# Accumulating DMAs for every third weight chunk only; VectorE subtracts for the others

## The chip, the cores and the metric

One core of one Trainium2 chip runs the whole program. The time is the device time of one execution in microseconds; the kernel before stands at a median of 909.94 us over three executions (907.95 to 910.76).

## What is computed

Three layers in a row on 2304 tokens of 512 features, all in float32. First random-feature attention with 8 heads of 64 features over 4 batches of 576 tokens, then a gated network, then a routed one with 8 experts (one for each token).

```python
q_p, k_p = (phi(q_s), phi(k_s))          # phi: exp(x @ omega.T - |x|^2/2 - max) / sqrt(128)
kv = np.einsum('bhsm,bhsd->bhmd', k_p, v)
num = np.einsum('bhsm,bhmd->bhsd', q_p, kv)      # divided by its normaliser
...
g = x @ w_gate                                   # w_gate, w_val: 512 x 1536, w_out: 1536 x 512
silu = g * (1.0 / (1.0 + np.exp(-g)))
val = x @ w_val
x = silu * val @ w_out
...
out[mask] = gate_w[mask, None] * (np.maximum(x[mask] @ w1[e], 0.0) @ w2[e])
```

The weights w_gate, w_val and w_out arrive as float64. "Chunk" means 128 rows by 512 columns of one of them; there are 36.

## The kernel before

*Precision.* A float32 product is made of three fast TensorE products: each operand is split in a high part, rounded to the engine's fast format (fp32r), and a low part, the rest (`mm3`, lines 169 to 171; `split`, lines 174 and 175). A weight chunk therefore needs a high and a low tile.

*Stages.* Tokens go in 6 groups of 3 tiles of 128. The first stage does three things at once: the attention of batch 0 and of the first group (16 "units" of one tile and four heads, of kind k or q), the conversion of all 36 weight chunks, and, as soon as the six q units are done, the gated network of group 0, together with 14 units for group 1. The gated network runs over f = 0 to 11 (128 hidden features each): 24 products into gv (four w_gate chunks, four w_val chunks), the gating (`gate`, lines 932 to 947, on ScalarE and VectorE), and 9 products into acc with a w_out chunk. f needs the chunks of its quarter f // 4. The other groups follow with the next group's units between their products, then the expert network in 10 slots.

*A chunk's steps* (`wsteps`, line 402). SP loads 512 KB of float64 into a w tile (line 400). Then a, b, c on VectorE (lines 414, 418, 422) put the bits of a float32 together out of the two integer halves, in a temporary tile t. d writes the high part, on VectorE for the first six chunks (line 428, NH = 6), on ScalarE for the others (line 430). e, on ScalarE, writes -t into the low tile, rounded (line 434). f, on GpSimd's queue, issues a DMA that adds t to the low tile (line 437), so that t minus its rounded value is left. The temporary t is one of three "row" buffers, or, for a "roomy" chunk (n % 5 >= 3 and n < 30, RM = (5, 3, 30)), a tile of the large pool "w" of 37. It is given back when the DMA has landed.

*The order.* Within the first stage it is planned ahead of time. `Plan` (line 84) holds steps with an engine, an assumed duration, the steps they wait for, the buffers they take and give, and a rank. `Plan.run` picks again and again the step that can start first by its own clock, and among those that start within 0.02 us the one with the lowest rank, and writes out its instructions. Every engine executes its own instructions in that order. The ranks are lines: chunk n has CR + CS n (23.68 + 8.39 n), its load CD + 1.4 n, a load waits for step c of the chunk WP = 5 before; the start's k units have 0 to 9 and q units RQ + RS i (7.83 + 1.56 i); the next group's unit i has UR + UD i (73.3 + 6.7 i); f has MR + MS f (44.22 + 15.56 f). The loads for the next group's units are issued by `pump`, first at rank PU = 2.0 and again each time a unit gives a load buffer back (`freed`, line 300). All loads are on SP's queue, in the planned order. The planner takes an accumulating DMA for 1.5 us and a lag of 2.4.

Behind the first stage the order comes from due times that don't depend on the plan. GpSimd also has the small bias operations (lines 536, 537) that the exponentials (line 546) wait for.

Of the kernel before, what the change touches and what calls it, by code (L numbers as in the profile page):

```python
# [8 lines left out]
F32 = mybir.dt.float32  # L9
# [3 lines left out]
ALU = mybir.AluOpType  # L13
# [15 lines left out]
FO = 5.72  # L29
FC = 0.6  # L30
MD = (0, 0, 0.17, 1.8, 2.18)
QL = -1.2
QD = 0.26
LAT = 0.34
GRAIN = 0.02
CR = 23.68
CD = -8.87
CS = 8.39
UR = 73.3
UD = 6.7  # L40
MR = 44.22
MS = 15.56
NH = 6
RR = 94.76
XL = 16.71
WU = 4
GF = 0
OR = 0
EO = 3.84
RQ = 7.83  # L50
RS = 1.56
PU = 2.0
WP = 5
RM = (5, 3, 30)
MXB = 4
US = 5.61
P = 128
# [64 lines left out]
def kernel(  # L122
# [16 lines left out]
    nc = tc.nc  # L139
# [33 lines left out]
    def split(src, hi, lo):  # L173
        nc.scalar.copy(hi, src)  # L174
        nc.vector.tensor_tensor(out=lo, in0=src, in1=hi.bitcast(F32), op=ALU.subtract)  # L175
# [7 lines left out]
    with tc.manual_schedule():  # L183
# [72 lines left out]
        def edge(t):  # L256

            return len(segs(t)) > 1
# [123 lines left out]
        wch = {}  # L382
# [9 lines left out]
        def wload(n):  # L392
            key = worder[n]
            r = wraw[key] = wpool.tile([P, DM, 2], I32, tag="w", name="wraw")
            if key[0] == "o":
                src = w_out[key[1] * P:(key[1] + 1) * P, :]
            else:
                src = (w_gate if key[0] == "g" else w_val)[
                    key[1] * P:(key[1] + 1) * P, key[2] * 4 * P:(key[2] + 1) * 4 * P]
            nc.sync.dma_start(out=r.rearrange("p c w -> p (c w)"), in_=src.bitcast(I32))  # L400

        def wsteps(key, by_dve, roomy):

            st = {}


            def a():
                st["r"] = wraw.pop(key)

                if roomy:  # L410
                    st["t"] = wpool.tile([P, 2 * DM], I32, tag="w", name="wt")[:, 0:DM]
                else:
                    st["t"] = rows.tile([P, DM], I32, tag="row", name="wt")
                nc.vector.tensor_scalar(out=st["t"], in0=st["r"][:, :, 1], scalar1=3, scalar2=0x3FFFFFFF,
                                        op0=ALU.logical_shift_left, op1=ALU.bitwise_and)

            def b():
                nc.vector.scalar_tensor_tensor(out=st["t"], in0=st["r"][:, :, 1], scalar=-0x40000000, in1=st["t"],
                                               op0=ALU.bitwise_and, op1=ALU.bitwise_or)

            def c():
                nc.vector.scalar_tensor_tensor(out=st["t"], in0=st["r"][:, :, 0], scalar=29, in1=st["t"],
                                               op0=ALU.logical_shift_right, op1=ALU.bitwise_or)

            def d():
                wch[key] = wpool.tile([P, 2, DM], F32R, tag="w", name="w")
                if by_dve:
                    nc.vector.tensor_copy(wch[key][:, 0, :], st["t"].bitcast(F32))
                else:
                    nc.scalar.copy(wch[key][:, 0, :], st["t"].bitcast(F32))  # L430


            def e():
                nc.scalar.mul(wch[key][:, 1, :], st["t"].bitcast(F32), -1.0)

            def f():
                nc.gpsimd.dma_start(out=wch[key][:, 1, :], in_=st["t"].bitcast(F32), accum_op=ALU.add)

            return a, b, c, d, e, f


        kv_sb = {}
# [274 lines left out]
        for g0, g1, nstat in ((0, NG - 1, 8), (NG - 1, NG, 2)):  # L717
# [3 lines left out]
            n = r.nt * P  # L721
# [431 lines left out]
        def start_unit(i, at, offs):  # L1153
            for n, f in unit_stages(i).items():
                T.at(at + offs[n], f)

        plan = Plan(dict(gv=2, acc=GT, misc=2, row=3, vt=4, h=2, xh=1, th=1, u=2, kvp=1, w=33),
                    dict(pe=LAT, act=LAT, dve=LAT, pool=LAT, dma=1.7, wadd=2.4))
        dur = dict(T=0.34, xh=0.26, sq=0.7, ss=0.42, pj=0.87, rd=0.7, md=0.4, ex=1.01, kv=0.83, ko=0.42, kw=0.43,
                    kp=0.42, qt=0.43, qc=0.39, nm=0.87, dv=1.09, xt=0.22, hi=0.27, lo=0.34)  # L1160
        on = dict(T="pe", xh="act", sq="act", pj="pe", rd="dve", ex="act", kv="pe", ko="act", kw="pe", kp="act", qt="pe", qc="act", nm="pe",
# [12 lines left out]
        def load_chunk(n):  # L1174
            back = chunk[n - WP][2] if n >= WP else None
            got["w", n] = plan.add("dma", 1.46, lambda: wload(n), [back], CD + 1.4 * n, ["w"])

        def load_q(n):
            loads[n] = first_x(n)
# [6 lines left out]
        where = {}  # L1186
        for n, key in enumerate(worder):
            load_chunk(n)
            roomy = n % RM[0] >= RM[1] and n < RM[2]
            st = wsteps(key, n < NH, roomy)  # L1190
            room1 = ["w" if roomy else "row"]
            c = []
            for f, (eng, d) in zip(st + (lambda: None,), (("dve", 0.34), ("dve", 0.61), ("dve", 0.61), ("dve", 0.34) if n < NH else ("act", 0.52), ("act", 0.53), ("pool", 0.9), ("wadd", 1.5))):
                c.append(plan.add(eng, d, f, [c[-1] if c else got["w", n]], CR + CS * n,
                                  room1 if f is st[0] else ["w"] if f is st[3] else [],
                                  ["w"] if f is st[2] else room1 if eng == "wadd" else []))
            chunk.append(c)
            where[key] = c[6]
        kvs = []
        ends = {}  # L1200
        on.update(sq="pool", ss="dve", md="pool")
# [3 lines left out]
        om_split = plan.add("act", 0.3, lambda: split(om_f, om_h, om_l), [], OR)  # L1205
        pumped = plan.add("dma", 1.6, pump, [got["edge", 1]], PU)
        for i in range(nu):
            kind, t, j = units[i]
            step = {"kvs": None, "kvt": None, "v": None}
            early = i < n_start  # L1210
            rank = UR + (i - n_start) * UD if not early else i if kind == "k" else RQ + RS * (i - 10)
            if not early:
                back = {k: ends[i - k] if i - k >= n_start else None for k in (2, 3)}
                step["x"] = plan.add("dma", 1.6, lambda: None, [back[3], pumped], rank)
            elif kind == "q":
                step["x"] = plan.add("dma", 0.8, lambda n=i: load_q(n), rank=QL + QD * (i - 10), take=["w"])
                step["kvs"], step["kvt"] = kvs[j]
# [6 lines left out]
            for n, f in unit_stages(i).items():  # L1224
                d = 0.43 if n == "kv" and edge(t) else dur[n]
                nd, eng = needs[n], on[n]
                if not early and n in ("sq", "md"):
                    nd, eng, d = (["T"], "act", 1.9) if n == "sq" else (["rd", "sq"], "pool", dur["md"])
                if not native and n == "pj":
                    nd, d = nd + [om_split], 0.65  # L1230
                if not native and n == "xh":
                    d = 0.6
# [26 lines left out]
        ra, rb, rc, rd = route_setup()  # L1259
        s = plan.add("dma", 0.5, later_loads, [s], XL)  # L1260
        s = plan.add("dve", 0.14, ra, [s], RR)
        s = plan.add("pe", 0.05, rb, [s], RR, ["misc"])
        s = plan.add("dve", 0.1, rc, [s], RR, [], ["misc"])
        plan.add("dve", 0.75, rd, [s], RR, [], ["w"])
        plan.run(ready[-1])
# [3 lines left out]
        for f in range(NF):  # L1269
            rank = MR + MS * f  # L1270
            s = half["v", 0] if f else ready[-1]
# [14 lines left out]
            if f:  # L1286
                s = half["v", 1]
                for i in range(GT):
                    s = plan.add("pe", 0.69, lambda f=f, i=i: l2(f - 1, i), [us[f - 1], where["o", f - 1, 0], s], rank,
                                 ["acc"] if f == 1 else [], ["u"] if i == GT - 1 else [])  # L1290
        plan.add("pe", 0.4, turn_gate, [], MR + 75)
        fin = plan.add("end", 0, lambda: None, [us[-1], s])
# [19 lines left out]
        st = slot_prefetch(A, 0, tf + PF, PD, tf + 2.6 * FO + FC * 11 + PG)  # L1312
        moe1_group(NG - 1)
        cur = pending[0]
        for i, (r, s) in enumerate(slots):
# [5 lines left out]
            st = nst  # L1321
# [57 lines left out]
```

## Time and profile before

| | us |
|---|---|
| median of three executions | 909.94 |
| profiled execution, device time | 909.23 |
| its span, first to last instruction | 907.5 |
| TensorE busy (matmul) | 866.2 |
| VectorE busy | 599.5 |
| ScalarE busy | 403.5 |
| GpSimd busy | 120.5 |

How to read it: "busy" counts the time in which at least one instruction of an engine runs. A view by stretch tells where an engine stood still, a view of waits names for each idle time the instruction that ended it (the one that ended it last by the records, which can be one that was itself held up), and the chain of work that ended last goes back from the end, at each step to what released it. PEclk is TensorE's granted clock as a share of 2.4 GHz. L414 means line 414; PE is TensorE, DVE VectorE, ACT ScalarE, POOL GpSimd. "w<-wt" is the accumulating DMA, "wraw<-in_..." a chunk's load.

### The profile page before, as it was taken

To read this page: it belongs to the slowest core of one execution; us is meant where nothing else is said; L and a number is where in the kernel's file an instruction comes from. 1 tells how busy PE (TensorE), PEld (TensorE's weight loads), DVE (VectorE), ACT (ScalarE), POOL (GpSimd) and SP (SyncE) were. 2 spreads that over 40 slices of the span, in tenths; PEclk is the share of its full clock that TensorE was granted. 3 is DMA by queue.
4 is the path that set the end of the run, shared out by engine and by line. 5 is a ranking of instruction groups with operands and counts; after the bars stand their busy time and mean duration, and the time that the engine had idled before them with its cause. 6 is when DMAs were issued, how large, how long until landed. Compare 5 with 4: busy or idle time off the path is not lost.

```text
span 907.5 us, 15212 instructions
## 1 busy us (share of the span) xinstructions
PE 866.2 (95%) x5320; PEld 799.5 (88%) x5320; DVE 599.5 (66%) x1535; ACT 403.5 (44%) x1101; POOL 120.5 (13%) x251
## 2 busy tenths in 40 slices
PE   7888689999999999999999999999999999999993
PEld 6777589999999999999999999999999999999992
DVE  5888558457665667655666665488787788766630
ACT  4777458543333334243343331112455555555520
POOL 6833133100000000000000000000201111112100
PEclk9999799999999999999999999999999999999997
DMA  9969894221222212222111111124587776676400
GB/s 266 268 160 263 205 263 85 42 63 43 59 76 63 55 35 53 47 81 55 35 42 45 45 28 36 47 82 140 163 325 251 243 238 223 221 236 216 137 19 22
DMA packets 96913, 112.89 MB, mean 124 GB/s; under 512 B 54176, under 2 KB 56242, under 8 KB 96827
## 3 DMA queue, kind: packets, MB, share of 16 engines
q1 hardware_dynamic: 88171, 92.35, 33.1%
q0 software_dynamic: 8384, 19.40, 9.2%
q8 instruction: 44, 0.72, 0.3%
q14 instruction: 42, 0.34, 0.1%
q10 hardware_dynamic: 272, 0.07, 0.0%
HBM read 92.91 MB, written 9.98 MB: 113 GB/s over the span
## 4 chain that ended last, share of the span: by engine, by line
PE 71%; issue 12%; DMA 9%; POOL 3%; DVE 2%; SPq 1%; ACT 1%; POOLq 0%; DVEq 0%
PE gv L169 10%; PE gv L171 10%; PE gv L170 10%; PE acc L169 7%; PE acc L170 7%; PE acc L171 7%; DMA w<-wt 3%; DMA out_dram<-orow,sidx 3%; PE num L601 3%; PE h L171 2%; PE h L170 2%; PE h L169 2%; DMA wraw<-in_moe_w_gate_dram 2%; PE kv L568 1%; PE qt L592 1%
## 5 line engine op out<-in xcount | busy, mean ns | idle before, releaser
L169 PE MATMUL gv<-xT,w 128*128 128x384 f32 x576 | 202.6, 352 | 2.8 <-DVE th L935 2.6
L171 PE MATMUL gv<-xT,w 128*128 128x384 f32 x576 | 194.8, 338 | 0.6 <-DMA w<-wt 0.6
L170 PE MATMUL gv<-xT,w 128*128 128x384 f32 x576 | 194.7, 338 | 0.0
L169 PE MATMUL acc<-w,uh 128*128 128x512 f32 x360 | 147.8, 410 | 0.0
L170 PE MATMUL acc<-w,uh 128*128 128x512 f32 x360 | 142.6, 396 | 0.0
L171 PE MATMUL acc<-w,ul 128*128 128x512 f32 x360 | 142.1, 395 | 0.0
L546 ACT ACTIVATE h<-pr,mx 128x128 f32<-128x128 f32 x224 | 63.9, 368 | 143.9 <-DVE mx L541 127.1
L169 PEld LDWEIGHTS gv<-xT,w 128*128 128x128 f32 x576 | 109.2, 190 | 7.7 <-DVE th L935 3.8
L170 PEld LDWEIGHTS gv<-xT,w 128*128 128x128 f32 x576 | 109.3, 190 | 2.9
L175 DVE TENSOR_TENSOR w<-raw,w 128x512 fp32r<-128x512 f32 x160 | 106.4, 686 | 6.1 <-ACT w L174 2.3
L171 PEld LDWEIGHTS gv<-xT,w 128*128 128x128 f32 x576 | 109.0, 189 | 0.9 <-DMA w<-wt 0.9
L747 DVE SCALAR_TENSOR_TENSOR wge<-xrow,wge 128x512 f32<-128x512 f32 x144 | 98.6, 684 | 10.1 <-DMA wge<-wg2t 9.5
L174 ACT CAST w<-raw 128x512 fp32r<-128x512 f32 x160 | 92.8, 617 | 4.6 <-DMA raw<-in_moe_w_dram 4.6
L169 PE MATMUL h<-sx,w 128*128 128x256 f32 x320 | 91.6, 286 | 0.0
L171 PE MATMUL h<-sx,w 128*128 128x256 f32 x320 | 90.5, 283 | 0.0
L170 PE MATMUL h<-sx,w 128*128 128x256 f32 x320 | 90.4, 283 | 0.0
L171 PEld LDWEIGHTS acc<-w,ul 128*128 128x128 f32 x360 | 68.0, 189 | 15.6 <-DVE ul L1095 0.2
L169 PEld LDWEIGHTS acc<-w,uh 128*128 128x128 f32 x360 | 68.5, 190 | 7.3
L170 PEld LDWEIGHTS acc<-w,uh 128*128 128x128 f32 x360 | 68.6, 190 | 7.0
L944 ACT CAST uh<-th 128x384 fp32r<-128x384 f32 x72 | 37.6, 522 | 67.5 <-DVE th L939 67.3
L525 DVE TENSOR_REDUCE mx<-pr 128x4 f32<-128x512 f32 x72 | 49.5, 688 | 26.1 <-PE pr L171 22.1
L169 PEld LDWEIGHTS h<-sx,w 128*128 128x128 f32 x320 | 61.0, 190 | 3.1
(196 smaller groups left out, 1434.7 us busy)
## 6 DMA issues: line engine op xcount, KB each, us to landing
raw<-in_moe_w_dram SPq DMA_DIRECT2D x80, 512.0 KB
wge<-wg2t SPq DMA_DIRECT2D x48, 256.0 KB
w<-wt POOLq DMA_DIRECT2D x36, 256.0 KB, 6.3
wraw<-in_moe_w_gate_dram SPq DMA_DIRECT2D x12, 512.0 KB
wraw<-in_moe_w_val_dram SPq DMA_DIRECT2D x12, 512.0 KB
wraw<-in_moe_w_out_dram SPq DMA_DIRECT2D x12, 512.0 KB
scr<-xrow SPq DMA_DIRECT2D x18, 256.0 KB
xin<-in_q_dram SPq DMA_DIRECT2D x26, 128.0 KB
```

The source lines that it names most:

```text
L169: nc.tensor.matmul(o, lh, rh, start=start, stop=False, skip_group_check=True)
L170: nc.tensor.matmul(o, lh, rl, start=False, stop=False, skip_group_check=True)
L171: nc.tensor.matmul(o, ll, rh, start=False, stop=stop, skip_group_check=True)
L174: nc.scalar.copy(hi, src)
L175: nc.vector.tensor_tensor(out=lo, in0=src, in1=hi.bitcast(F32), op=ALU.subtract)
L525: nc.vector.tensor_reduce(out=mx, in_=pr, axis=AX.X, op=ALU.max)
L546: nc.scalar.activation(out=h[:, a, :], in_=pr[:, a, :], func=ACTF.Exp, bias=mx[:, a:a + 1])
L568: nc.tensor.matmul(kv_ps[0][:, g, :], h[:, c, :], vt[:, c, 0:D + 1], start=t == own[0] and c == 0, stop=t == own[-1], skip_group_check=True)
L592: nc.tensor.transpose(qt[:, h, :], st["h"][:, h, :], ident)
L601: nc.tensor.matmul(num[r:r + m, h, :], st["h"][:, h, r:r + m], kv_sb[b, j][:, h, :], start=True, stop=True)
L747: nc.vector.scalar_tensor_tensor(out=st[e][:, 1, :], in0=xrows[i], scalar=1.0, in1=st[e][:, 0, :], op0=ALU.mult, op1=ALU.mult, accum_out=L ...
L944: nc.scalar.copy(u[f][0], th[f])
```

## The change

For chunks with n % 3 = 1 (12 of 36) all steps stay as they are, with the high part on ScalarE. For the other 24, steps e and f fall away, and VectorE writes the low part as t minus the high part ("low"). Temporary tiles out of the w pool are now for accumulating chunks with n < 30 only (ten of them); a temporary tile of a chunk without a DMA is given back behind "low". The high part is on ScalarE for all chunks. The planner's assumed lag of the DMA goes from 2.4 to 3.0, and the ranks of the first stage have other values.

```diff
--- before.py
+++ after.py
@@ -29,29 +29,28 @@
 FO = 5.72
 FC = 0.6
 MD = (0, 0, 0.17, 1.8, 2.18)
-QL = -1.2
-QD = 0.26
+QL = -1.24
+QD = 0.41
 LAT = 0.34
 GRAIN = 0.02
-CR = 23.68
-CD = -8.87
-CS = 8.39
-UR = 73.3
-UD = 6.7
-MR = 44.22
-MS = 15.56
-NH = 6
-RR = 94.76
-XL = 16.71
+CR = -3.19
+CD = -8.51
+CS = 8.62
+UR = 68.99
+UD = 9.09
+MR = 46.53
+MS = 29.47
+RR = 106.64
+XL = 17.9
 WU = 4
 GF = 0
 OR = 0
 EO = 3.84
-RQ = 7.83
-RS = 1.56
-PU = 2.0
+RQ = 7.32
+RS = 2.67
+PU = 9.84
 WP = 5
-RM = (5, 3, 30)
+RM = (3, 1, 30)
 MXB = 4
 US = 5.61
 P = 128
@@ -399,7 +398,7 @@
                     key[1] * P:(key[1] + 1) * P, key[2] * 4 * P:(key[2] + 1) * 4 * P]
             nc.sync.dma_start(out=r.rearrange("p c w -> p (c w)"), in_=src.bitcast(I32))
 
-        def wsteps(key, by_dve, roomy):
+        def wsteps(key, by_dma, roomy):
 
             st = {}
 
@@ -424,10 +423,11 @@
 
             def d():
                 wch[key] = wpool.tile([P, 2, DM], F32R, tag="w", name="w")
-                if by_dve:
-                    nc.vector.tensor_copy(wch[key][:, 0, :], st["t"].bitcast(F32))
-                else:
-                    nc.scalar.copy(wch[key][:, 0, :], st["t"].bitcast(F32))
+                nc.scalar.copy(wch[key][:, 0, :], st["t"].bitcast(F32))
+
+            def low():
+                nc.vector.tensor_tensor(out=wch[key][:, 1, :], in0=st["t"].bitcast(F32),
+                                        in1=wch[key][:, 0, :].bitcast(F32), op=ALU.subtract)
 
 
             def e():
@@ -436,7 +436,7 @@
             def f():
                 nc.gpsimd.dma_start(out=wch[key][:, 1, :], in_=st["t"].bitcast(F32), accum_op=ALU.add)
 
-            return a, b, c, d, e, f
+            return (a, b, c, d, e, f, lambda: None) if by_dma else (a, b, c, d, low)
 
 
         kv_sb = {}
@@ -1155,7 +1155,7 @@
                 T.at(at + offs[n], f)
 
         plan = Plan(dict(gv=2, acc=GT, misc=2, row=3, vt=4, h=2, xh=1, th=1, u=2, kvp=1, w=33),
-                    dict(pe=LAT, act=LAT, dve=LAT, pool=LAT, dma=1.7, wadd=2.4))
+                    dict(pe=LAT, act=LAT, dve=LAT, pool=LAT, dma=1.7, wadd=3.0))
         dur = dict(T=0.34, xh=0.26, sq=0.7, ss=0.42, pj=0.87, rd=0.7, md=0.4, ex=1.01, kv=0.83, ko=0.42, kw=0.43,
                     kp=0.42, qt=0.43, qc=0.39, nm=0.87, dv=1.09, xt=0.22, hi=0.27, lo=0.34)
         on = dict(T="pe", xh="act", sq="act", pj="pe", rd="dve", ex="act", kv="pe", ko="act", kw="pe", kp="act", qt="pe", qc="act", nm="pe",
@@ -1186,16 +1186,19 @@
         where = {}
         for n, key in enumerate(worder):
             load_chunk(n)
-            roomy = n % RM[0] >= RM[1] and n < RM[2]
-            st = wsteps(key, n < NH, roomy)
+            by_dma = n % RM[0] == RM[1]
+            roomy = by_dma and n < RM[2]
+            st = wsteps(key, by_dma, roomy)
             room1 = ["w" if roomy else "row"]
             c = []
-            for f, (eng, d) in zip(st + (lambda: None,), (("dve", 0.34), ("dve", 0.61), ("dve", 0.61), ("dve", 0.34) if n < NH else ("act", 0.52), ("act", 0.53), ("pool", 0.9), ("wadd", 1.5))):
+            on_w = [("dve", 0.34), ("dve", 0.61), ("dve", 0.61), ("act", 0.52)]
+            on_w += [("act", 0.53), ("pool", 0.9), ("wadd", 1.5)] if by_dma else [("dve", 0.61)]
+            for f, (eng, d) in zip(st, on_w):
                 c.append(plan.add(eng, d, f, [c[-1] if c else got["w", n]], CR + CS * n,
                                   room1 if f is st[0] else ["w"] if f is st[3] else [],
-                                  ["w"] if f is st[2] else room1 if eng == "wadd" else []))
+                                  ["w"] if f is st[2] else room1 if f is st[-1] else []))
             chunk.append(c)
-            where[key] = c[6]
+            where[key] = c[-1]
         kvs = []
         ends = {}
         on.update(sq="pool", ss="dve", md="pool")
```

## Rows read from the trace of the kernel before

**Rows 1.** Busy time by stretch: us, each engine's busy us, granted clock, DMA share.
```profile
0.00:182.00 182.00, 156.38 (x933) 138.84 (x934) 125.48 (x278) 114.47 (x386) 74.14 (x180) 0.95 0.77 193
8.00:60.00 52.00, 42.84 (x270) 35.76 (x269) 42.99 (x98) 37.34 (x130) 36.06 (x98) 0.99 0.91 231
8.00:131.00 123.00, 101.24 (x579) 88.10 (x579) 92.30 (x197) 78.01 (x262) 58.09 (x135) 0.93 0.93 242
60.00:90.00 30.00, 27.52 (x159) 25.49 (x158) 24.29 (x48) 18.74 (x56) 11.31 (x17) 0.97 0.95 254
93.70:100.30 6.60, 0.00 (x1) 0.00 (x0) 2.55 (x7) 0.09 (x1) 0.39 (x2) 0.68 1.11 254
100.30:107.00 6.70, 6.68 (x25) 6.11 (x26) 4.42 (x12) 4.30 (x17) 0.10 (x1) 0.55 0.59 112
125.60:131.00 5.40, 5.37 (x24) 4.91 (x25) 2.76 (x5) 3.82 (x12) 1.45 (x3) 0.68 1.05 360
131.00:182.00 51.00, 50.87 (x342) 47.23 (x342) 31.30 (x72) 33.38 (x118) 12.29 (x24) 1.00 0.39 71
182.00:880.00 698.00, 698.00 (x4324) 650.55 (x4323) 471.70 (x1251) 287.16 (x711) 44.37 (x69) 1.00 0.35 111
```

**Rows 2.** Waits of TensorE, 59.9 to 182 us: total us, times, longest.
```profile
PE xt L483 <- DVE setup L690: 6.6, 1, 6.6
PE gv L169 <- DVE th L935: 2.6, 3, 1.2
PE pr L169 <- DVE xl L175: 2.3, 1, 2.3
PE gv L171 <- DMA w<-wt: 0.6, 1, 0.6
```

**Rows 3.** VectorE in order of time: start, length, idle time before and its releaser.
```profile
97.75 0.76 DVE L414 TENSOR_SCALAR wt<-wraw 128x512 int32<-128x512 int32 x2 [6.96 <-DMA w<-wt]
...
122.42 0.43 DVE L414 TENSOR_SCALAR wt<-wraw 128x512 int32<-128x512 int32 x1 [1.92 <-DMA w<-wt]
```

**Rows 4.** Chain of work that ended last: start us, length us, what.
```profile
85.99 11.73 DMA w<-wt
```

**Rows 5.** Groups of instructions, 0 to 182 us: count, busy us, mean ns, idle before.
```profile
L437 POOL DMA_DIRECT2D w<-wt x36 | 31.9, 952 | 28.9 <-ACT w L434 25.9 <-issue 0.9 <-ACT xT L623 0.7
...
L422 DVE SCALAR_TENSOR_TENSOR wt<-wraw,wt 128x512 int32<-128x512 int32 x36 | 25.5, 712 | 0.1
...
L418 DVE SCALAR_TENSOR_TENSOR wt<-wraw,wt 128x512 int32<-128x512 int32 x36 | 24.5, 684 | 0.2
...
L434 ACT ACTIVATE w<-wt 128x512 fp32r<-128x512 f32 x36 | 22.7, 652 | 0.0
...
L430 ACT CAST w<-wt 128x512 fp32r<-128x512 f32 x30 | 18.1, 635 | 5.6 <-DVE wt L422 5.6
...
L414 DVE TENSOR_SCALAR wt<-wraw 128x512 int32<-128x512 int32 x36 | 15.9, 454 | 17.2 <-DMA w<-wt 14.5 <-DMA wraw<-in_moe_w_val_dram 2.8
...
L428 DVE CAST w<-wt 128x512 fp32r<-128x512 f32 x6 | 2.5, 412 | 0.0
```

**Rows 6.** Group of instructions in the page: the expert weights' subtraction.
```profile
L175 DVE TENSOR_TENSOR w<-raw,w 128x512 fp32r<-128x512 f32 x160 | 106.4, 686 | 6.1 <-ACT w L174 2.3
```

**Rows 7.** Waits of VectorE for ScalarE, 182 to 907 us.
```profile
DVE xl L175 <- ACT xh L174: 36.4, 35, 2.1
...
DVE w L175 <- ACT w L174: 2.3, 2, 1.3
```

**Rows 8.** SP's DMA issues in order of time around its gap.
```profile
85.39 0.87 SPq L400 DMA_DIRECT2D wraw<-in_moe_w_gate_dram  x1
...
103.79 0.38 SPq L253 DMA_DIRECT2D xin<-in_k_dram  x1
```

**Rows 9.** GpSimd in order of time, two equal products.
```profile
32.81 0.61 POOL L497 TENSOR_TENSOR first<-first 128x256 f32<-128x256 f32 x1
...
34.99 0.91 POOL L497 TENSOR_TENSOR first<-first 128x256 f32<-128x256 f32 x1
```

## The prediction

> **What bounds the kernel now.** I read the busy time by stretch first [rows 1]. From 182 to 880 us TensorE is busy for 698.00 of 698.00 us at a granted clock of 1.00, so behind 182 us only less TensorE work would help, and the edit doesn't touch that: it changes the planner's input, and the planner writes out only the first stage, whose last matmul ends at 182 us. Between 131 and 182 us TensorE is busy too (50.87 of 51.00 us). Whatever there is to win lies before 131 us: it stands still for all of 93.7 to 100.3 us and for 2.5 of the 30 us from 60 to 90, and the clock is 0.55 and 0.68 of full speed in two stretches, each just behind a standstill: a mix of 2.4 GHz and 1.2 GHz.
>
> Next the list of TensorE's waits from 59.9 to 182 us [rows 2]: 6.6, 2.6, 2.3 and 0.6 us, 12.1 in all. The name beside the largest (VectorE's setup, line 690) is not its cause. VectorE's queue [rows 3] shows a chunk's first step (line 414) that starts at 97.75 us after 6.96 us of waiting for an accumulating DMA; line 690 and a row maximum merely stood behind it. The chain of waits [rows 4] has that DMA with 11.73 us from 85.99. The mechanism is the row buffer: three of them, each held by a chunk until its accumulation has landed, and VectorE runs in order. The 2.3 us are of the same kind: a step of line 414 waits 1.92 us up to 122.42 [rows 3], and the xl that TensorE needs comes after it.
>
> A slow clock costs 6.70 x 0.45 = 3.0 us, 5.40 x 0.32 = 1.7 and 30 x 0.03 = 0.9 [rows 1], together 5.6. So TensorE alone could end the stage at 182 - 12.1 - 5.6 = 164.3 us. Of these 17.7 us, 6.6 + 2.3 + 0.6 + 3.0 + 1.7 = 14.2 go back to accumulating DMAs.
>
> **The change part by part.** *Accumulations.* 24 of 36 go (chunks with n % 3 = 1 keep theirs). With each goes a negation on ScalarE and an issue on GpSimd: 24 x 0.652 = 15.6 us and 24 x 0.952 = 22.8 us [rows 5]. On GpSimd's queue stand the small bias operations that the exponentials wait for, so they come forward; what that is worth before 60 us I bound below. A chunk without a DMA gives its row buffer back when VectorE itself has subtracted, so the next line 414 never waits for another engine on its account. Of the 12 accumulating chunks ten now take a w tile (n < 30), and only n = 31 and 34 hold a row buffer. A third of 14.2 us would be 4.7; as two chunks of 12 can still block a row, I leave 2 us of it in the time, between 0 and 4.7.
>
> *VectorE.* The subtraction isn't in the trace for these tiles; the same one, 128x512 fp32r out of two SBUF operands, takes 0.686 us 160 times later on [rows 6]. 24 x 0.686 = 16.5 us come; six hi copies of 0.412 [rows 5], 2.5 us, move to ScalarE, where they take 0.635 each. VectorE's work up to 182 us grows from 125.5 [rows 1] to 139.5 us. None of that is hidden for certain: VectorE is the engine that takes over the bound. In 8 to 131 us it is idle for 123 - 92.3 = 30.7 us [rows 1]; line 414's waits for the accumulation and for one load explain 14.5 + 2.8 [rows 5], and 13.4, or 11%, are left as ordinary gaps. With 11% gaps the new work ends at 8 + 139.5 / 0.89 = 164.7 us, as good as TensorE's 164.3. At the occupancy of 8 to 60 us, 42.99 of 52 or 83%, it would be 8 + 139.5 / 0.83 = 176.
>
> *The new wait.* Each subtraction waits for ScalarE's hi copy of its chunk. Behind it on VectorE stand the next chunks, the row maxima and the gating of the first expert network, so GpSimd, ScalarE and TensorE wait for it in turn. The nearest pairs: the same copy and subtraction in the later stages cost 2.3 us for 160 pairs, 0.01 each, and xl behind its xh in the steady stage 36.4 us over 35 waits, 1.04 each, where VectorE has time to spare [rows 7]. I take 0.15 each, near the lower end, as the planner puts other work between copy and subtraction: 24 x 0.15 = 3.6 us, between 0.2 and 25.
>
> *The start, up to 60 us.* The rank of chunk 0 falls from 23.68 to -3.19, so chunks 0 to 2 (-3.19, 5.43, 14.05) may go ahead of attention units (0 to 9, and 7.32 to 20.67). Price: at most three chunks of 0.454 + 0.684 + 0.712 + 0.686 = 2.5 us, 7.6 us of VectorE [rows 5, 6], of which idle time (17% of the stretch) takes some. Against it GpSimd, busy for 36.06 of the 52 us [rows 1], loses two in three of its 0.952 us issues there. I bound the sum by 4 us either way and take 0.
>
> *Ranks and load order.* Units of the next group now go ahead of f of the expert network earlier (29.47 per f, before 15.56), and the pump of their loads stands behind some six more chunk loads (9.84, before 2.0, at 1.4 per chunk). On SP's queue a unit's load can hold the chunk loads behind it: between 85.39 and 103.79 us it issued nothing [rows 8]. VectorE lost only 2.8 us to a chunk load so far [rows 5]; between a gain of 2.8 and the 17.5 us of that blockade I take 0, since most of the chunks are on chip before they are wanted.
>
> *Sum.* 164.5 + 3.6 + 2 = 170.1 us for the end of the stage, 12 us before 182. The profiled execution took 909.23 us (span 907.5 and 1.73 around it; 0.7 under the median of 909.94): 909.23 - 12 = 897.
>
> *A rule that speaks against it.* GpSimd's 128x256 product takes 0.61 us at 32.81 us and 0.91 at 34.99, while VectorE converts a chunk [rows 9]. The Trainium skill (page "SBUF — State Buffer", section "SBUF: two separate sides") says why that can be: a VectorE operation with two SBUF inputs and a GpSimd operation that reads SBUF exclude one another for the whole instruction. The new subtraction has two SBUF inputs, so the rule would have each of the 24 hold GpSimd back by up to its length, an estimated 2 us on the path if one in eight hits a bias operation, and the sum would be 899 instead of 897.
>
> **The rivals.**
> - TensorE alone is left as the bound: the subtractions never wait, and the start gains its 4 us. For it: both ends come to 164.5 us already. Against it: VectorE would have to run at 139.5 of 156 us, 89%, throughout. 909.23 - 17.7 - 2 to 4 = 888.
> - VectorE waits for ScalarE (slower). In-order VectorE stands at each subtraction until ScalarE, itself held by exponentials that wait for GpSimd and so for VectorE's row maxima, has copied. At the 1.04 us of xl [rows 7] the stage ends at 164.5 + 25 + 2 = 191.5, 9.5 us later: 919. It decides from (182 - 164.5 - 2) / 24 = 0.65 us a subtraction. For it: VectorE loses its slack. Against it: 0.01 us in 160 equal pairs.
> - The loads give it back (no change). SP's blockade of 17.5 us [rows 8] moves to where VectorE has emptied the stock of loaded chunks; 12 to 15 us of that come back, 907 to 910. For it: chunks are used up faster, their loads don't start faster. Against it: 2.8 us so far.
> - The edit does what it says in any case: the 24 issues are absent from the program. What may not come is the release of the row buffers, if chunks 31 and 34 alone block as before; that is the 4.7 us above.
>
> **How the numbers follow.** Forecast (stage ends at 165 to 179 us) 0.61; TensorE alone 0.14; VectorE waits 0.15; loads 0.10. 0.3%, 2.7 us, is about what a measurement of this kernel tells from no change. Faster: 0.61 + 0.14 = 0.75; the loads case gives 0.08 to no change and 0.02 to slower; slower 0.17. The range runs from the first rival with the start's 4 us (909.23 - 17.7 - 4 = 887) to the middle of the loads case, 908: 0.61 + 0.14 + half of 0.10 = 0.80.
>
> **What would show it.** Right: line 414 no longer waits for the accumulation by more than about 2 us in sum; no standstill of TensorE over 3 us behind 60 us; clock near 1.00 throughout the stage; VectorE busy for about 139 us in it; last matmul of group 0 at about 170 us, and the rest as long as before. Wrong: VectorE's subtractions wait for ScalarE by more than 0.65 us each (second rival); line 414 waits for chunk loads by 10 us or more (third); TensorE begins the expert network clearly after 60 us, so that the start pays for the new ranks; or the stretch behind the stage changes its length.

## The result and the profile after

The changed kernel takes 893.99 us (median of four, 893.12 to 895.30) where the kernel before takes 910.2: a ratio of 0.9828, 95% interval 0.9806 to 0.9849. The profiled execution takes 894.53 us with a span of 892.8, against 909.23 and 907.5: 14.7 us less.

The busy time by stretch divides these 14.7 us (columns as in [rows 1]). First the kernel before, cut where TensorE begins the first step of the next stage, a transposition of line 483 (182.89 us), and where its last product ends (891.86):

```profile
0.00:182.89 182.89, 157.27 (x937) 139.55 (x938) 125.60 (x279) 114.84 (x387) 74.14 (x180) 0.95 0.77 192
182.89:891.86 708.97, 708.96 (x4384) 659.90 (x4382) 472.85 (x1253) 288.63 (x714) 45.36 (x70) 1.00 0.35 109
891.86:907.50 15.64, 0.00 (x0) 0.00 (x0) 1.03 (x4) 0.00 (x0) 0.98 (x1) 0.59 0.06 15
```

And the changed kernel, cut at the same two steps:

```profile
0.00:170.46 170.46, 154.84 (x937) 138.05 (x938) 136.07 (x297) 106.04 (x369) 56.76 (x156) 0.98 0.62 170
170.46:879.59 709.13, 709.13 (x4384) 660.20 (x4382) 472.88 (x1252) 288.66 (x714) 46.33 (x70) 1.00 0.35 109
879.59:892.80 13.21, 0.00 (x0) 0.00 (x0) 1.03 (x4) 0.00 (x0) 0.98 (x1) 0.62 0.06 18
```

The first stage ends at 170.46 instead of 182.89 us, 12.4 us earlier. What TensorE does behind it has kept its length, 708.97 and 709.13 us. The rest, 15.64 us before and 13.21 now, lies behind the last product; these 2.4 us stood in no step of the prediction.

Inside the first stage, the stretches that answer to [rows 1]:

```profile
8.00:60.00 52.00, 45.02 (x273) 38.12 (x272) 42.38 (x95) 37.29 (x130) 30.88 (x92) 0.97 0.71 202
8.00:131.00 123.00, 111.28 (x670) 98.50 (x669) 108.28 (x232) 82.15 (x294) 49.01 (x125) 0.97 0.74 206
60.00:90.00 30.00, 27.90 (x164) 25.76 (x163) 26.64 (x57) 16.41 (x62) 6.53 (x12) 0.94 0.77 203
```

VectorE is busy for 108.28 of the 123 us from 8 to 131, where it was 92.30. TensorE is busy for 111.28 instead of 101.24. The long standstill has gone, though from 60 to 90 us the granted clock is 0.94 where it was 0.97. TensorE's waits from 59.5 us to the end of the stage, against the 12.1 us of [rows 2], now sum to 4.3:

```profile
PE gv L168 <- DVE th L935: 2.0, 1, 2.0
PE qt L592 <- ACT h L546: 1.1, 1, 1.1
PE gv L168 <- DVE th L939: 0.9, 1, 0.9
PE pr L168 <- ACT xh L173: 0.3, 1, 0.3
```

The groups of instructions that answer to [rows 5] (lines of the changed kernel; line 413 was 414, 429 is the new subtraction, 426 the hi copy):

```profile
L421 DVE SCALAR_TENSOR_TENSOR wt<-wraw,wt 128x512 int32<-128x512 int32 x36 | 25.6, 714 | 0.0
...
L417 DVE SCALAR_TENSOR_TENSOR wt<-wraw,wt 128x512 int32<-128x512 int32 x36 | 24.3, 681 | 0.0
...
L426 ACT CAST w<-wt 128x512 fp32r<-128x512 f32 x36 | 22.3, 633 | 4.9 <-DVE wt L421 4.7
...
L429 DVE TENSOR_TENSOR w<-wt,w 128x512 fp32r<-128x512 f32 x24 | 16.2, 684 | 0.0
...
L413 DVE TENSOR_SCALAR wt<-wraw 128x512 int32<-128x512 int32 x36 | 14.7, 429 | 0.0
...
L437 POOL DMA_DIRECT2D w<-wt x12 | 10.9, 904 | 7.7 <-DVE wt L413 3.1 <-ACT w L434 2.8 <-issue 1.1
...
L434 ACT ACTIVATE w<-wt 128x512 fp32r<-128x512 f32 x12 | 7.9, 655 | 0.0
```

Line 413 had 17.2 us of idle time before it, 14.5 of them for accumulations; it has none now. The subtractions, 24 of 0.684 us, have none either.

### The profile page after: what moved, and what is told of

Its sections match the earlier page's. It is cut to its first block, busy times and chain, and to the rows that moved or that the text cites. A ratio compares the mean times of both kernels' runs of the same rounds, so it can differ in the third digit from the quotient of the medians.

```text
span 892.8 us, 15148 instructions
## 1 busy us (share of the span) xinstructions
PE 864.0 (97%) x5320; PEld 798.3 (89%) x5320; DVE 610.0 (68%) x1553; ACT 394.7 (44%) x1083; POOL 104.1 (12%) x227
## 4 chain that ended last, share of the span: by engine, by line
PE 83%; DVE 7%; issue 4%; DMA 2%; POOL 2%; ACT 1%; POOLq 0%; DVEq 0%; ACTq 0%
PE gv L168 11%; PE gv L170 10%; PE gv L169 10%; PE acc L168 9%; PE acc L169 9%; PE acc L170 9%; PE h L170 4%; PE h L169 4%; PE h L168 4%; PE num L601 3%; PE kv L568 2%; PE qt L592 2%; DMA out_dram<-orow,sidx 2%; DVE wt L417 1%; PE xt L483 1%
## 5 line engine op out<-in xcount | busy, mean ns | idle before, releaser
L546 ACT ACTIVATE h<-pr,mx 128x128 f32<-128x128 f32 x224 | 63.9, 369 | 139.5 <-DVE mx L541 127.9
L935 DVE SCALAR_TENSOR_TENSOR th<-th,gv 128x384 f32<-128x384 f32 x72 | 39.6, 550 | 37.5 <-ACT th L932 37.5
```

The source lines that it names most:

```text
L546: nc.scalar.activation(out=h[:, a, :], in_=pr[:, a, :], func=ACTF.Exp, bias=mx[:, a:a + 1])
L935: nc.vector.scalar_tensor_tensor(out=th[f], in0=th[f], scalar=1.0, in1=ps.pop((f, "g")), op0=ALU.add, op1=ALU.mult)
```

## The experiments

Two of the edits, step b left out and the subtraction made twice, leave the planner's input alone, and these two kernels keep the changed kernel's order. Every other edit feeds the planner, so that kernel has its own order in the first stage. The table puts them side by side by their profiled executions: number of accumulating DMAs, median time, ratio to the kernel before with its 95% interval, first product of the gated network (the end of the start), first square of the group after (the end of the stage; 0.6 to 0.7 us behind the cut above), and what lies behind TensorE's last product. The last three columns are us of the profiled execution, which can lie some us beside the median.

| kernel | accum. | us | ratio (interval) | first product | next stage | rest |
|---|---|---|---|---|---|---|
| before | 36 | 909 to 910 | 1 | 59.96 | 183.6 | 15.64 |
| changed | 12 | 893.99 | 0.9828 (0.9806 to 0.9849) | 59.52 | 171.1 | 13.21 |
| swap, old ranks | 12 | 893.67 | 0.9844 (0.9819 to 0.9869) | 57.60 | 170.3 | 13.06 |
| new ranks alone | 36 | 917.38 | 1.0085 (1.0057 to 1.0113) | 63.78 | 192.9 | 15.64 |
| before, w tiles | 36 | 907.26 | 0.9982 (0.9963 to 1.0001) | 61.69 | 180.1 | 15.35 |
| none accumulates | 0 | 891.10 | 0.9807 (0.9790 to 0.9824) | 57.55 | 168.2 | 11.84 |
| half accumulates | 18 | 896.06 | 0.9867 (0.9837 to 0.9896) | 61.43 | 171.0 | 13.74 |
| step b left out | 12 | 888.33 | 0.9775 (0.9759 to 0.9792) | 59.62 | 164.5 | 13.02 |
| subtracted twice | 12 | 904.18 | 0.9953 (0.9936 to 0.9970) | 61.60 | 181.2 | 13.16 |
| 12 in row buffers | 12 | 912.64 | 1.0044 (1.0028 to 1.0061) | 61.80 | 188.9 | 13.16 |
| GpSimd subtracts 12 | 0 | 897.18 | 0.9859 (0.9843 to 0.9876) | 63.55 | 175.2 | 11.87 |
| 12 negations back | 0 | 892.34 | 0.9812 (0.9798 to 0.9827) | 58.71 | 170.1 | 11.96 |
| none, old ranks | 0 | 889.14 | 0.9774 (0.9761 to 0.9787) | 56.96 | 167.0 | 11.99 |
| GpSimd fills 12 | 0 | 896.46 | 0.9853 (0.9837 to 0.9869) | 60.28 | 176.6 | 12.06 |

**The swap or the new order.** The diff does two things at once. The swap with all fourteen ranks of the kernel before, and with its 2.4 for the lag of an accumulation:

```diff
-CR = -3.19
+CR = 23.68
...
-                    dict(pe=LAT, act=LAT, dve=LAT, pool=LAT, dma=1.7, wadd=3.0))
+                    dict(pe=LAT, act=LAT, dve=LAT, pool=LAT, dma=1.7, wadd=2.4))
```

> The swap alone: 24 accumulating DMAs replaced by VectorE's subtraction, temporary tiles as in the changed kernel, but every rank and the assumed lag of the kernel before. Theory A (the gain is the row buffer that no longer waits for a DMA to land): line 414's waits for the accumulation fall from 14.5 us to under 3, TensorE's standstill of 6.6 us is gone, 897 to 902 us. Theory B (the gain is the new order of the first stage): 905 to 912 us, with standstills over 3 us left.

893.67 us, below the 897 to 902 of theory A: the whole gain is there without one new rank. Line 413 no longer waits for an accumulation at all; the waits of VectorE for ScalarE's copy and for another DMA are what is left of the kind (first stage; columns as in [rows 7]):

```profile
DVE w L429 <- ACT w L426: 1.6, 2, 1.3
...
DVE wt L413 <- DMA wg2t<-ws: 0.6, 1, 0.6
```

And the fourteen ranks and the lag alone, in the kernel before:

```diff
-CR = 23.68
+CR = -3.19
...
-                    dict(pe=LAT, act=LAT, dve=LAT, pool=LAT, dma=1.7, wadd=2.4))
+                    dict(pe=LAT, act=LAT, dve=LAT, pool=LAT, dma=1.7, wadd=3.0))
```

> The new ranks and the assumed lag alone: all 36 chunks still accumulate by DMA, in the buffers of the kernel before. Theory A: line 414 goes on waiting for accumulations by 10 us or more, 905 to 912 us. Theory B: 894 to 900 us.

917.38 us, slower than before by 0.85% and outside both ranges. I had expected no change or a gain. The start takes 3.8 us longer, and line 414's waits for accumulations grow from 14.5 to 19.9 us:

```profile
DVE wt L414 <- DMA w<-wt: 19.9, 10, 3.8
```

So the new order isn't what makes the kernel faster. With the swap it makes no difference that is clear of noise (893.99 and 893.67); without the swap it costs.

**The row buffer, from both sides.** First the changed kernel with all twelve accumulations that are left in row buffers:

```diff
-RM = (3, 1, 30)
+RM = (3, 1, 0)
```

> The changed kernel, but all 12 accumulating chunks hold a row buffer until the DMA has landed, none a tile of the w pool. Theory A: line 414 waits for accumulations again, 2 to 6 us in sum, 895 to 899 us. If the number of accumulations matters and not the buffer: 893 to 895.

912.64 us. Nothing but the place of twelve temporaries (and the order that follows) differs, and the gain is gone and more. My upper end was 899. VectorE's waits in the first stage, then the stretches behind the start:

```profile
DVE wt L413 <- DMA w<-wt: 16.0, 5, 4.2
```

```profile
60.00:131.00 71.00, 65.42 (x389) 59.86 (x390) 60.40 (x126) 44.71 (x174) 12.90 (x34) 0.93 0.69 191
131.00:188.00 57.00, 49.01 (x269) 43.13 (x269) 33.12 (x71) 23.19 (x73) 5.73 (x12) 0.88 0.28 66
```

Five waits of a chunk's first step for a landing, 16.0 us, and the stage ends at 188.9 instead of 171.1 us. TensorE is busy for 65.42 of 71 and 49.01 of 57 us, and the granted clock is 0.93 and 0.88: the standstills cost time twice, once as such (5.6 + 8.0 us) and once by the share of 1.2 GHz in the mix behind them (71 x 0.07 + 57 x 0.12 = 11.8 us, by the prediction's way of counting), as in the fifth and sixth of the stretches of [rows 1].

The number of accumulations in row buffers doesn't scale this by itself: the kernel before had 24 of them there (and 12 in w tiles), and line 414 waited 14.5 us; here 12 make 16.0 us. With three (half accumulates) and two (changed) there is no such wait.

Then the other way round, the kernel before with w tiles for the temporaries of chunks 0 to 29:

```diff
-RM = (5, 3, 30)
+RM = (1, 0, 30)
```

> The kernel before with all 36 accumulations, but chunks 0 to 29 all put their temporary into a tile of the w pool, so that almost none holds a row buffer. Theory A: line 414's waits fall from 14.5 us to under 5 and TensorE's 6.6 us standstill goes, 898 to 905 us (unless w tiles run short and loads wait instead). If it is not the row buffer but the DMAs themselves (their engines, GpSimd's issues, ScalarE's negations) that cost: 907 to 912 us.

907.26 us, a ratio whose interval reaches from 0.9963 to 1.0001: undecided, and at best a fifth of the gain. It lies in the range that I had given the DMAs themselves, 907 to 912. VectorE's waits, then SP's, then TensorE's largest wait behind the start:

```profile
DVE wt L414 <- DMA wraw<-in_moe_w_out_dram: 5.0, 1, 5.0
DVE wt L414 <- DMA w<-wt: 4.2, 4, 1.4
```

```profile
SPq L400 <- DMA w<-wt: 16.8, 4, 6.9
```

```profile
PE kv L568 <- ACT h L546: 6.2, 1, 6.2
```

Line 414's waits for accumulations fall from 14.5 to 4.2 us as expected, but TensorE has a standstill of 6.2 us, nearly as long as the one in [rows 2], at another place. It goes back to a chunk's load, for which line 414 waits 5.03 us up to 98.13; a row maximum, GpSimd's bias operations and the exponential stand behind it. The chain of work that ended last has that load (start and length), and the stretch from 60 to 131 us shows what it stood among:

```profile
83.15 14.52 DMA wraw<-in_moe_w_out_dram
```

```profile
60.00:131.00 71.00, 61.66 (x350) 56.91 (x351) 55.82 (x115) 47.09 (x159) 23.34 (x41) 0.93 1.00 267
```

The load took 14.52 us to land, while the 16 DMA engines were busy throughout (share 1.00; 0.77 in the changed kernel, where loads of this stretch take 4.6 to 5.2 us in the middle). SP also waits 16.8 us for w tiles that accumulations still hold, but nearly all of that comes after this load was issued, so it isn't what made it late. That the accumulations made the landing slow is likely and not shown. Free row buffers alone therefore don't give the gain while all 36 accumulations stay, and fewer accumulations alone don't either (912.64). The changed kernel does both.

**Is VectorE the new bound?** Less work on it, then more. Without step b, line 417, for the 24 chunks, which leaves the sign bits out of their weights:

```diff
             def b():
+                if not by_dma:
+                    return
```

> The changed kernel without step b (line 417) for the 24 chunks that VectorE subtracts: their sign bits are left out of the weights, so that part of the computation is missing. 24 x 0.681 = 16.3 us less on VectorE, all else as it is. If VectorE bounds the stage: most of the 6.6 us that TensorE still loses behind 60 us comes back, 887 to 890 us. If VectorE has slack: 893 to 895 us.

888.33 us, 5.7 under the changed kernel. And each subtraction made twice:

```diff
             def low():
                 nc.vector.tensor_tensor(out=wch[key][:, 1, :], in0=st["t"].bitcast(F32),
                                         in1=wch[key][:, 0, :].bitcast(F32), op=ALU.subtract)
+                nc.vector.tensor_tensor(out=wch[key][:, 1, :], in0=st["t"].bitcast(F32),
+                                        in1=wch[key][:, 0, :].bitcast(F32), op=ALU.subtract)
```

> The changed kernel with each of the 24 subtractions made twice: 16.4 us more on VectorE, no new wait for another engine. If VectorE bounds the stage: 10 to 17 us slower, 904 to 911 us. If it has slack of its own, about 3 us or less: 894 to 897.

904.18 us, 10.2 above. The stretch from 60 to 131 us in the changed kernel, without step b, and with two subtractions (each its own answer):

```profile
60.00:131.00 71.00, 66.26 (x399) 60.38 (x398) 65.90 (x138) 44.86 (x165) 18.13 (x33) 0.98 0.77 210
```

```profile
60.00:131.00 71.00, 70.57 (x451) 65.89 (x451) 63.90 (x136) 50.22 (x184) 15.00 (x36) 0.99 0.79 221
```

```profile
60.00:131.00 71.00, 62.52 (x352) 56.04 (x353) 66.72 (x132) 42.21 (x159) 16.04 (x31) 0.91 0.68 192
```

TensorE is busy for 66.26, 70.57 and 62.52 of 71 us. 16.3 us less on VectorE end the stage 6.6 us earlier, 16.4 us more end it 10.1 us later: VectorE is part of the bound, with 0.4 us of the stage for each us taken off it and 0.6 for each put on. Without step b, this is all that TensorE waits for from its first product to the end of the stage (columns as in [rows 2]):

```profile
PE qt L594 <- ACT h L548: 0.2, 1, 0.2
```

So there is no more to be had from VectorE there: the 104.9 us from 59.6 to 164.5 are TensorE's own.

**What the twelve that are left cost.** No accumulation at all, VectorE subtracts everywhere:

```diff
-            by_dma = n % RM[0] == RM[1]
+            by_dma = False
```

> The changed kernel with no accumulating DMA at all: 12 more subtractions of 0.684 us, 8.2 us more on VectorE, 12 negations and 12 issues less. If VectorE is now the bound of the first stage: 5 to 9 us slower than the changed kernel, 899 to 903 us. If TensorE or the start bounds it: 893 to 896. If the 12 accumulations left still cost what I charged them (2 us): 891 to 893.

891.10 us. Not slower by 5 to 9 us, as a VectorE bound alone would have it, but 2.9 us faster, although the intervals of the two ratios overlap a little. VectorE's 8.2 us more are there (68.23 of 71 us busy), and TensorE loses less:

```profile
60.00:131.00 71.00, 68.97 (x436) 63.33 (x435) 68.23 (x143) 44.37 (x172) 11.12 (x26) 1.00 0.57 183
```

The two profiled executions are 3.8 us apart. The stage ends 2.9 us earlier, 2.0 of them before the first product (57.55 and 59.52 us), and 1.4 lie behind TensorE's last product. So each of the twelve costs about what a subtraction costs in its place, or more, though no row buffer waits for one. Eighteen instead of twelve:

```diff
-RM = (3, 1, 30)
+RM = (2, 1, 30)
```

> The changed kernel with every second chunk accumulating (18 instead of 12; 15 of them in w tiles, 3 in row buffers): 4.1 us less on VectorE. If VectorE bounds the stage: 890 to 893 us. If accumulations cost by themselves, about 0.4 us each as in the kernel before (14.2 us for 36): 895 to 898 us. If neither: 893 to 895.

896.06 us: what VectorE is spared (4.1 us) doesn't come back, which fits a cost of their own, but this interval and the changed kernel's overlap as well.

Which part of an accumulation costs? The negation on ScalarE put back, without a DMA:

```diff
-            return (a, b, c, d, e, f, lambda: None) if by_dma else (a, b, c, d, low)
+            return (a, b, c, d, e, low) if by_dma else (a, b, c, d, low)
...
-            roomy = by_dma and n < RM[2]
+            roomy = False
...
```

> The kernel without accumulations, with the 12 negations put back on ScalarE (12 x 0.655 = 7.9 us) ahead of the subtraction that overwrites what they write. C3: 893 to 895 us, the gain of leaving out the 12 accumulations is gone. C1 or C2: 890 to 892 us.

892.34 us, a ratio of 0.9812 beside 0.9807: not the negation. GpSimd in place of the DMA:

```diff
+            def low_pool():
+                nc.gpsimd.tensor_tensor(out=wch[key][:, 1, :], in0=st["t"].bitcast(F32),
+                                        in1=wch[key][:, 0, :].bitcast(F32), op=ALU.subtract)
...
-            return (a, b, c, d, e, f, lambda: None) if by_dma else (a, b, c, d, low)
+            return (a, b, c, d, low_pool) if by_dma else (a, b, c, d, low)
...
```

> The changed kernel with GpSimd subtracting for the 12 chunks that still accumulate: no accumulating DMA and no negation is left, VectorE does the same as in the changed kernel, and GpSimd is busy for them at least as long as with the 12 issues (10.9 us there; twice the 0.6 to 0.7 us of its 128x256 product, an estimate of 14 to 17 us). Theory C1 (an accumulation costs through its landing, since a buffer or a product waits for it): the kernel without accumulations stands at 891.1 us, 8.2 us less on VectorE takes 2 to 5 us more off, 886 to 889 us. Theory C2 (it costs GpSimd's time, for which the bias operations wait): 893 to 897 us. Theory C3 (it costs ScalarE's negation): as C1.

897.18 us, with nothing left that lands: clearly slower than without accumulations, and no faster than with the twelve DMAs (these two intervals just overlap). GpSimd's groups show a subtraction of 1.511 us, 18.1 us in all, where the twelve issues took 10.9:

```profile
L434 POOL TENSOR_TENSOR w<-wt,w 128x512 fp32r<-128x512 f32 x12 | 18.1, 1511 | 12.1 <-ACT w L426 12.1
```

To have less of it, GpSimd only fills the low tile, which VectorE then overwrites:

```diff
+            def fill():
+                nc.gpsimd.memset(wch[key][:, 1, :].bitcast(F32), 0.0)
...
-            return (a, b, c, d, e, f, lambda: None) if by_dma else (a, b, c, d, low)
+            return (a, b, c, d, fill, low) if by_dma else (a, b, c, d, low)
...
-            roomy = by_dma and n < RM[2]
+            roomy = False
...
```

> The kernel without accumulations, in which GpSimd fills the low tile of every third chunk with zeros before VectorE's subtraction overwrites it: 12 fills of 128x512 in place of the 12 issues, by the 0.20 us of the 128x128 fill an estimate of 0.8 us each, 10 us of GpSimd, with no DMA, no negation and no landing. C2 (an accumulation costs GpSimd's time): 893 to 896 us, most of the 2.9 us between the changed kernel (893.99) and the one without accumulations (891.1) is lost again, above all before the first product of the expert network at 57.55 us. C1 (landing): 890.5 to 892 us.

896.46 us, 5.4 more than without them, by fills that take 6.2 us:

```profile
L434 POOL MEMSET w<- 128x512 f32 x12 | 6.2, 525 | 0.0
```

Both speak for GpSimd's queue (theory C2), though each comes out just above the upper end of its range, and against the landing: where nothing lands, the time still rises as soon as a chunk goes by GpSimd. The stage ends 7.0 us later with the subtractions, 6.0 of them before the first product (63.55 and 57.55 us). With the fills it ends 8.4 us later, 2.7 of them before the first product; but that profiled execution, at 898.88 us, is the slowest of its five, 2.4 above the median, so the 5.4 us between the medians are the better measure, and they are no more than the fills are long. Here the subtraction also stands behind the fill, and the planner's order is another one each time. How much is GpSimd's time, how much the wait for its queue and how much the order is not settled by these runs.

**The version that beats both.** No accumulation, and the fourteen ranks and the lag of the kernel before:

```diff
-CR = -3.19
+CR = 23.68
...
-            by_dma = n % RM[0] == RM[1]
+            by_dma = False
```

> The kernel without accumulations with the ranks of the kernel before. If the ranks are neutral once no row buffer waits for a DMA, as between the changed kernel and the swap alone (893.99 and 893.67 us): 890 to 893 us. If the new ranks suit a planner without accumulations: 894 us or more.

889.14 us, 0.9774 (0.9761 to 0.9787), clear of the changed kernel's interval and, barely, of that of the same kernel with the new ranks (0.9790 to 0.9824). The start is the shortest of all (56.96 us), and TensorE's two largest sums of waits behind it are these:

```profile
PE gv L168 <- DVE th L935: 3.1, 3, 1.2
PE kv L568 <- ACT h L546: 1.3, 1, 1.3
```

The 3.1 us are waits for the gating (line 935), which stands behind other work in VectorE's queue.

## Why the prediction was right

The forecast was 897 us in a range of 887 to 908, and faster; it is 894.0. By its own steps:

- *Where the bound lies.* Right. Behind the stage TensorE's stretch kept its length to 0.2 us, and 12.4 of the 14.7 us are in the first stage.
- *The mechanism, the row buffer.* Right, and stronger than I put it. The swap without the new ranks gives the gain, and back in row buffers twelve accumulations cost 18.7 us. I left 2 us in the time for the twelve, between 0 and 4.7; their row waits are 0 in the changed kernel, since ten hold w tiles, and 16.0 us when they don't. That the diff keeps them in w tiles was a condition of the gain, not a remark beside it. "A third of the loss" was the wrong way to scale it: 24 in row buffers made 14.5 us of waits, 12 made 16.0. What the prediction left out is the traffic of the accumulations: with all 36 of them and hardly a wait for a row buffer, a standstill came back behind a load that took 14.52 us. How the 12.4 us divide between the rows, the traffic and GpSimd's 21.0 us less of issues (31.9 and 10.9), no run shows.
- *The end of the stage.* 170.1 us was the sum, against 182; 170.46 is measured, against 182.89 at the same step, so 11.9 us earlier were forecast and 12.4 came. That it fits so closely is in part luck. The terms: VectorE's ordinary gaps 11%, measured (123 - 108.28) / 123 = 12%; its work 139.5 us, measured 136.07, as line 413 takes 14.7 us instead of 15.9 and operations overlap more. The wait of the subtraction for ScalarE was 3.6 us in the sum and is 0 in the trace: the step was mis-sized, and what stands in its place is a part of the 6.1 us that TensorE still loses (4.3 of waits, and 30 x 0.06 = 1.8 of clock from 60 to 90 us). The prediction took 164.5 us for two ends that lay 0.4 us apart, TensorE's and VectorE's, as if the one would hide in the other; the doses of 0.4 and 0.6 us for one show that neither bounds alone. That interplay had no term of its own.
- *The twelve that are left.* Too low in another way: by the medians they cost 2.9 us more than subtracting in their place (the intervals overlap), and that isn't the row buffer; a part is the time behind the last product. I priced the 24 issues that go on GpSimd's queue, and not the twelve that stay.
- *The start.* Taken as 0 within 4 us; 59.52 instead of 59.96 us.
- *Ranks and load order.* Taken as 0; right together with the swap, since the same swap with the old ranks takes as long. Alone the ranks cost 8 us. That lies inside the bound of 17.5 us that I gave them through the loads, but it comes another way: line 414 waits 19.9 us for accumulations, and the start is 3.8 us longer.
- *A VectorE bound as the price.* Confirmed by both doses, though by 0.4 to 0.6 us for one, not one for one.
- *The rest behind the stage.* Wrong. "The rest as long as before" missed 2.4 us behind the last product. Without it the time would have been about 896.4, within 1 us of the forecast; so the step that failed is an assumption, not the sum. Of the signs that I named for right, the clock missed too: 0.94 from 60 to 90 us is not near 1.00.
- *The rivals.* VectorE waiting for ScalarE's copy: no such idle time. Loads: no wait of VectorE for a DMA is left in the first stage. SP does wait once, 8.8 us, for a w tile that an accumulation holds, and no chunk comes late for it. TensorE alone: not reached, 6.1 us short of it; the kernel without step b, where TensorE waits for 0.2 us, shows what it would be.

The rule that I weighed speaks of GpSimd and VectorE excluding one another. The product at 34.99 us that I quoted for it is no instance: beside it VectorE runs line 414, which reads one tile (34.99 to 36.18 us, 1.19 where its mean is 0.454), and line 422, with two inputs, for the first 0.09 us only. The bias operations are a better test, lines 536 and 537, in the kernel before, then in the changed one (groups of instructions, 0 to 182 us):

```profile
L536 POOL TENSOR_TENSOR mx<-ss,mx 128x4 f32<-128x4 f32 x30 | 9.5, 315 | 49.6 <-DVE mx L525 45.2 <-ACT w L430 3.3
...
L537 POOL TENSOR_TENSOR mx<-mx,ss 128x4 f32<-128x4 f32 x30 | 8.8, 292 | 2.4
```

```profile
L536 POOL TENSOR_TENSOR mx<-ss,mx 128x4 f32<-128x4 f32 x30 | 15.0, 499 | 68.4 <-DVE mx L525 52.8 <-ACT h L500 6.3 <-ACT w L426 4.6
...
L537 POOL TENSOR_TENSOR mx<-mx,ss 128x4 f32<-128x4 f32 x30 | 8.7, 290 | 2.4
```

Line 536 takes 0.499 instead of 0.315 us on the mean, while VectorE makes 24 more operations with two SBUF inputs; line 537 stays as it was. The two lines together take 18.3 us before, 23.7 in the changed kernel, 18.1 where step b, which also has two SBUF inputs, is left out 24 times, and 23.2 with each subtraction made twice; with twelve accumulations in row buffers they take 18.9, although VectorE makes the same operations as in the changed kernel. That agrees in part with the Trainium skill (page "SBUF — State Buffer", section "SBUF: two separate sides"), by which such an operation and a GpSimd operation that reads SBUF shut one another out. The 5.5 us are GpSimd's; that they moved the end of the stage no run here shows.

## What to carry to other kernels

A DMA in the middle of a chain of small steps can cost more by the buffer that it holds until it has landed than by its own length: the same twelve cost 18.7 us more in scarce buffers. Look for the engine that runs in order and needs that buffer next, and move the hold to buffers of which there are enough, or do the step on an engine that is in the chain anyway. Moving the hold alone may not do: with 36 such DMAs the next limit was a load that landed late among them. Where a wait list names an unlikely releaser, look at what stood ahead of it in that releaser's own queue. And measure a swap and the order that was planned around it apart: here one gave everything and the other, alone, a loss.

## What the runs showed of the hardware

The time between TensorE's last product and the end of the execution goes with how many accumulating DMAs GpSimd issued hundreds of microseconds earlier. It is 15.35 to 15.64 us with 36 of them, 13.74 with 18, 13.02 to 13.21 with 12 and 11.84 to 12.06 with none, in the profiled executions of fourteen kernels, about 0.10 us for each. The last instructions of the engines there are the same ones in the kernel before, in the changed one and with none or eighteen. What fills the time isn't seen in the trace, so its cause stays open; it made 2.4 of the 14.7 us.

A 256 KB accumulation from SBUF into SBUF lands later, the more of them there are: 5.6 to 6.3 us in the middle with 36 in the stage (three kernels), 5.0 with 18, 3.4 to 4.8 with 12 (five kernels). From the issue to the landing, in the kernel before and in the changed one (line 437):

```profile
DMA to landing us min/median/max: 3.3/6.3/12.2
```

```profile
DMA to landing us min/median/max: 3.3/4.1/9.4
```
